# The product of probabilities and values with V held in the array: four 32-column strips instead of eight weight loads, and 64-row scores

## The chip, the cores and the metric

The kernel runs on one core of a Trainium2 chip. The metric is the device time of one launch in microseconds (us). Unless ns is written, all times here are in us. TensorE multiplies (PE in the profile; PEld are its weight loads), ScalarE evaluates exponentials (ACT), VectorE (DVE) and GpSimd (POOL) do the rest of the arithmetic, SyncE (SP) and POOL issue the transfers.

## The reference, cut to what matters

A transformer block with adaptive layer norm and its whole backward pass: 2048 tokens, width 512, 32 heads of 16, a hidden layer of 1792. The change touches the forward attention alone:

```python
H = 32
Dh = D // H
qkv = (x @ wqkv).reshape(B, S, 3, H, Dh).transpose(2, 0, 3, 1, 4)
q, k, v = qkv[0], qkv[1], qkv[2]
scores = einsum('bhqd,bhkd->bhqk', q, k) * Dh ** -0.5
p = softmax(scores, axis=-1)
o = einsum('bhqk,bhkd->bhqd', p, v)
return o.transpose(0, 2, 1, 3).reshape(B, S, D) @ wo
```

The forward also has `x + ga * A(h)`, a second norm, `r = relu(h @ w1 + b1)`, `(r * r) @ w2 + b2`; then come the gradients of all inputs and weights.

## The kernel before, in words

**Stages.** `phase_fwd` holds the whole forward and the part of the backward that goes by token (the MLP gradients); `phase5` is the backward attention; `phase6` the last weight gradients. PE and SP follow the order in which the program is written throughout; in the forward loop ACT and DVE do too. POOL does so in the opening, and is ordered by the scheduler from the second part of the loop on.

**Tiling of the forward attention.** Queries are cut into four chunks of 512 (`qc`), the 32 heads into eight groups of four (`g`), a group into two pairs (`jp`), and the keys into sixteen blocks of 128 (`kb`). One pair, one key block and one query chunk make a *unit*: 1024 units in all. A unit is

- two score matmuls (L388, or L354 in the opening): the 128 keys of a block are the stationary operand (`KTq`, four heads in four 32-row strips, each 16 rows of head and 16 of zeros), the 512 queries of one head move (`QTm`, all rows but those of the head zero). The result is one tile `st` of two PSUM banks; there are two such tiles, so the scores of a unit wait until ACT has read those of the unit two before;
- one exponential over both heads on ACT (L391, L357), 128 partitions by 1024, into `pu`, of which there are six;
- eight matmuls with `pu` stationary (L322, `pv`): each loads 128 by 128 of `pu` and moves 17 columns of `Vaug` (16 of V and one of ones, which gives the softmax's sum). The result has tokens on partitions: 2 heads by 4 token tiles by 17 columns of one bank, `accbank`, of which there are two.

After a pair's last block, two reciprocals (L329) and two multiplications (L330) on DVE turn `accbank` into rows of `O32`.

**What sets the order.** `pend` holds the eight-matmul products of past units; a unit may execute those that are two units old. Beside them the *background* runs: generators that emit one matmul per `yield` (queries and keys of the next group in chunk 0, `gen_qkv`; the MLP of the chunk before, `gen_mlp`, in chunks 1 to 3). `Background.step` adds a rate (1.2 in chunk 0, 1.14 later) to a credit and runs matmuls while the credit is positive; a generator can ask for a hold of some units with `("wait", n)`. `room` (L398) lets fewer products run in a unit that has more background. `bg.until(mark)` runs background up to a mark at once.

**Loads.** `load_q` (L299) issues two DMAs on POOL's queue that refill the queries of the next pair in the one set of four `QTm` tiles; a refill waits for the score matmuls that still read the tile. `load_k` does so for the keys.

**The opening** (L339 to L364) lays the first group's 32 units between the norm, the projections and the transposes that they need (`gen_open`). Its first queries lie in two extra tiles `QTo`.

**The end of the loop.** After the last unit the rest of `pend` runs (L419), `take_o` (L1156) casts `O32` to bf16, and `last_chunk` does the fourth chunk's MLP, forward and backward, with PE as the engine that is kept full. What background is left (three quarters of the second MLP product of chunk 2, `fc2`, L1255 and the bias L1257) is laid in by `bg.take` and, at L828, by `bg.drain()`, before the transposes of the second norm's output (L782) and the first MLP product (L838).

Of the kernel before, what the change touches and what calls it, by code (L numbers as in the profile page):

```python
# [9 lines left out]
BF16 = mybir.dt.bfloat16  # L10
F32 = mybir.dt.float32
ACT = mybir.ActivationFunctionType
ALU = mybir.AluOpType
AX = mybir.AxisListType
PSUM = bass.MemoryType.PSUM
# [4 lines left out]
P = 128  # L20
DH = 16
# [14 lines left out]
class Background:  # L36
# [13 lines left out]
    def next(self):  # L50
        while self.gens:
            r = next(self.gens[0], None)
            if r is not None:
                if isinstance(r, tuple):
                    self.mark = r[0]
                    self.seen.add(r[0])
                return r
            self.gens.pop(0)
        return None

    def plan(self, rate):
        return 0 if self.hold or not self.gens else max(0, math.ceil(min(self.credit + rate, 2.0)))

    def step(self, rate):
        if self.hold:
            self.hold -= 1
            return
        self.credit = min(self.credit + rate, 2.0)
        while self.gens and self.credit > 0:
            r = self.next()  # L70
            if r is None:
                break
            if isinstance(r, tuple):
                self.hold = r[1]
                break
            self.credit -= max(r, 0.25)

    def until(self, mark):
        while mark not in self.seen:
# [26 lines left out]
class K:  # L106
# [160 lines left out]
    def phase_fwd(self):  # L267
# [5 lines left out]
        tc, nc, pp = self.tc, self.nc, self.pp  # L273
# [15 lines left out]
        fw = self.open_pool("fw", bufs=1)  # L289
# [2 lines left out]
        pup = self.open_pool("fwp", bufs=6)  # L292
        self.mps = self.open_pool("mps", bufs=2, space=PSUM)
        stp = self.open_pool("fwst", bufs=2, space=PSUM)
        accp = self.open_pool("fwacc", bufs=2, space=PSUM)
        O32 = self.ra.tile([P, 4, D], F32, name="O32")
        QTm = [fw.tile([P, 512], BF16, name=f"QTm{j}") for j in range(4)]

        def load_q(qc, g, jp):  # L299
            with tc.high_priority():  # L300
                for j in (2 * jp, 2 * jp + 1):
                    nc.gpsimd.dma_start(QTm[j][32 * j:32 * j + 32, :], self.QTq_d[g, 32 * j:32 * j + 32, 512 * qc:512 * (qc + 1)])  # L302

        def load_k(qc, g):
            if qc == 0:
                return self.KT_next
            t = kp.tile([P, S], BF16, name="KTq")
            with tc.high_priority():
                nc.gpsimd.dma_start(t[:], self.KTq_d[g])
            return t  # L310

        SPAN, PVT = 4.15, 0.12
        order = [(qc, g, jp) for qc in range(SC) for g in range(NQ) for jp in range(2)]
        bg = Background()
        bg.add(self.gen_qkv(kp))
        pend = []

        def pv(w):
            (u, a, sub) = w
            (n, qc, g, jp, kb, acc, pu) = u  # L320
            h = 4 * g + 2 * jp + a
            nc.tensor.matmul(acc[:, a, sub, :], lhsT=pu[:, a, sub * P:(sub + 1) * P], rhs=Vaug[:, kb, h, :],  # L322
                             start=(kb == 0 and a == 0 and sub == 0), stop=False, skip_group_check=True)
            if kb < ST - 1 or (a, sub) != (1, 3):
                return
            st0 = 4 * qc
            for a in range(2):
                h = 4 * g + 2 * jp + a
                nc.vector.reciprocal(self.rl[:, st0:st0 + 4, h], acc[:, a, :, DH])  # L329
                nc.vector.tensor_tensor(O32[:, :, h * DH:(h + 1) * DH], acc[:, a, :, 0:DH],  # L330
                                        self.rl[:, st0:st0 + 4, h:h + 1].to_broadcast([P, 4, DH]), ALU.mult)
            if (g, jp) == (NQ - 1, 1) and qc < SC - 1:
                bg.add(self.gen_mlp(qc, self.take_o(qc, O32)))

        KT = kp.tile([P, S], BF16, name="KTq")
        self.late = []
        self.cur_g = 0
        es = ExitStack()
        es.enter_context(tc.manual_schedule(engines=ALL))  # L339
        QTo = []  # L340
        first = self.gen_open(Vaug, KT, QTm, QTo, stp, bg)
        next(first)
        accs = []
        for n in range(2):
            accb = accp.tile([P, 512], F32, name="accbank")
            accs.append(accb[:, 0:8 * (DH + 1)].rearrange("p (a s e) -> p a s e", a=2, s=4))
        units = [(n, 4 * s + k) for s in range(SC) for n in range(2) for k in range(4)]
        for i, (n, kb) in enumerate(units):
            if i == len(units) // 2:
                bg.until(1)  # L350
                load_q(*order[2])
            stt = stp.tile([P, 2, 512], F32, name="st")
            for a in range(2):
                nc.tensor.matmul(stt[:, a, :], lhsT=KT[:, kb * P:(kb + 1) * P], rhs=(QTm[2 + a] if n else QTo[a])[:],  # L354
                                 start=True, stop=True)
            pu = pup.tile([P, 2, 512], BF16, name="pu")
            nc.scalar.activation(pu[:], stt[:], ACT.Exp, scale=self.scale)  # L357
            u = (n, 0, 0, n, kb, accs[n], pu)
            next(first)
            pend.extend((u, a, sub) for a in range(2) for sub in range(4))  # L360
            while len(pend) > 24:
                pv(pend.pop(0))
        next(first)
        es.close()  # L364
# [1 line left out]
        late, self.late = self.late, None  # L366
        bg.until(-1)
        KT = self.KT_next
        for n, (qc, g, jp) in list(enumerate(order))[2:]:
            if (qc, g, jp) == (1, 0, 0):  # L370
                bg.drain()
                es.close()
                self.close_qkv()
                self.open_mlp()
                bg.add(self.gen_weights())
            accb = accp.tile([P, 512], F32, name="accbank")
            acc = accb[:, 0:8 * (DH + 1)].rearrange("p (a s e) -> p a s e", a=2, s=4)
            self.cur_g = g
            for kb in range(ST):
                if kb == (5 if qc == 0 and jp == 1 else 1) and n + 1 < len(order):  # L380
                    if n < 2 * NQ - 1 and jp == 1:
                        bg.until(g + 1)
                    load_q(*order[n + 1])
                    if jp == 1:
                        KTn = load_k(*order[n + 1][:2])
                stt = stp.tile([P, 2, 512], F32, name="st")
                for a in range(2):
                    nc.tensor.matmul(stt[:, a, :], lhsT=KT[:, kb * P:(kb + 1) * P], rhs=QTm[2 * jp + a][:],  # L388
                                     start=True, stop=True)
                pu = pup.tile([P, 2, 512], BF16, name="pu")  # L390
                nc.scalar.activation(pu[:], stt[:], ACT.Exp, scale=self.scale)  # L391
                u = (n, qc, g, jp, kb, acc, pu)
                now = n * ST + kb
                pend.extend((u, a, sub) for a in range(2) for sub in range(4))
                if late:
                    late.pop(0)()
                rate = 1.14 if qc else 1.2
                room = int((SPAN - 2 - bg.plan(rate)) / PVT)  # L398
                while pend:
                    age = now - max(pend[0][0][0] * ST + pend[0][0][4], 2 * ST - 2)  # L400
                    if age < 2 or (room <= 0 and age < 4):
                        break
                    pv(pend.pop(0))
                    room -= 1
                bg.step(rate)
            if jp == 1 and n + 1 < len(order):
                if n < 2 * NQ - 1:
                    bg.until(-(g + 1))
                KT = KTn
        bg.until(f"fc2_{SC - 2}")  # L410
# [4 lines left out]
        for k in range(2):  # L415
            t = self.mk.tile([P, D], BF16, name="x0", bufs=2)
            nc.gpsimd.dma_start(t[:], self.io["A_x"][0].rearrange("(st p) d -> p st d", p=P)[:, ST - 4 + k, :])
            x0s.append(t)
        while pend:  # L419
            pv(pend.pop(0))  # L420
        O_b = self.take_o(SC - 1, O32)
        for name in ("fwacc", "fwst", "fwp", "fwk", "fw"):
            self.close_pool(name)
        self.last_chunk(bg, O_b, x0s, O32)

    def gen_open(self, Vaug, KT, QTm, QTo, stp, bg):

        tc, nc, io = self.tc, self.nc, self.io
        S, D, H, NQ, ST, DT, SC = self.S, self.D, self.H, self.NQ, self.ST, self.DT, self.SC
# [32 lines left out]
            load_x(s4)  # L462
        nc.sync.dma_start(self.wmod[:, :, 2 * D:6 * D], wmod_v[:, :, 2 * D:6 * D])
        nc.gpsimd.memset(Vaug[:, :, :, DH:DH + 1], 1.0)
        nc.vector.memset(QTm[0][:], 0.0)
        self.silu_c(ps)
        QTo.extend(sa_.tile([P, 512], BF16, name=f"QTo{j}") for j in range(2))
        for t in QTo + QTm[1:]:
            nc.vector.memset(t[:], 0.0)
        for t in self.wpad0 + wpads[::-1]:  # L470
            nc.scalar.memzero(t[:])
# [1 line left out]
        def warm(n):  # L473
            w = stp.tile([P, 2, 512], F32, name="st")
            for _ in range(n):
                nc.tensor.matmul(w[:, 0, :], lhsT=self.ones_b[:], rhs=QTm[0][:], start=True, stop=True)

        warm(12)
        xhat1 = tokens("auT", "xhat1")
# [54 lines left out]
        def fm(*a, **k):  # L534
            for _ in self.gen_fm(ps, *a, **k):
                pass
# [22 lines left out]
        warm(4)  # L559
        fm(1, 0, 0, dst=KT[:, 0:512])  # L560
        pad0(0)
        fm(0, 0, 0, masked=QTo + QTm[2:])
        warm(2)
        for st in range(4, 8):
            stat(st)
# [1393 lines left out]
```

## Time and profile before

| what | us |
|---|---|
| median of 3 runs | 2509.76 (2506.19 to 2510.69) |
| the profiled execution: its time, its span | 2511.14, 2509.0 |
| opening up to the first exponential | 16.7 |
| opening, 32 units | 47.5 |
| chunk 0, the other 224 units | 208.1 |
| chunk 1, 256 units | 238.4 |
| chunk 2, 256 units | 235.3 |
| chunk 3, 256 units | 235.5 |
| last chunk's MLP and the dense weight gradients (from 981.5 to 1170) | 188.5 |
| backward attention (1170 to 2400) | 1230 |
| rest | 109 |

The stages were cut at the starts of exponentials, read from the timeline. A profile shows one execution. A row of the groups has the source line, the engine, the operation, output and inputs, shape, count, then busy time and mean duration of one. Matmuls overlap in the array, so a mean of 377 ns does not say that one starts every 377 ns: starts are read from the timeline. The granted clock of TensorE was 1.00 in nearly all stages, 0.99 in chunk 1.

### The profile page before, as it was taken

To read this page: it belongs to the slowest core of one execution; us is meant where nothing else is said; L and a number is where in the kernel's file an instruction comes from. 1 tells how busy PE (TensorE), PEld (TensorE's weight loads), DVE (VectorE), ACT (ScalarE), POOL (GpSimd) and SP (SyncE) were. 2 spreads that over 40 slices of the span, in tenths; PEclk is the share of its full clock that TensorE was granted. 3 is DMA by queue.
4 is the path that set the end of the run, shared out by engine and by line. 5 is a ranking of instruction groups with operands and counts; after the bars stand their busy time and mean duration, and the time that the engine had idled before them with its cause. 6 is when DMAs were issued, how large, how long until landed. Compare 5 with 4: busy or idle time off the path is not lost.

```text
span 2509.0 us, 68721 instructions
## 1 busy us (share of the span) xinstructions
PE 2438.6 (97%) x26695; PEld 1080.0 (43%) x26695; DVE 1709.6 (68%) x3519; ACT 2295.0 (91%) x3789; POOL 716.4 (29%) x1289
## 2 busy tenths in 40 slices
PE   8999999999999999999999999999999999999998
PEld 4555555555555554573333333333333333333343
DVE  6222322422332344677999999999999999999957
ACT  7999999999999997534999999999999999999935
POOL 2344531220131022245222222222222222222223
PEclk9999999999999999999999999999999999999999
DMA  4688661441243044598999999999999999999997
GB/s 166 133 180 208 170 121 50 129 100 39 99 115 90 23 131 138 122 199 214 236 215 227 224 221 228 223 222 221 229 222 222 230 223 222 225 226 232 233 191 208
DMA packets 1260526, 445.78 MB, mean 178 GB/s; under 512 B 1204052, under 2 KB 1228246, under 8 KB 1260198
## 3 DMA queue, kind: packets, MB, share of 16 engines
q1 hardware_dynamic: 1219654, 336.29, 70.7%
q0 software_dynamic: 38464, 104.04, 13.6%
q8 instruction: 209, 3.42, 0.6%
q10 hardware_dynamic: 2080, 1.05, 0.1%
q14 instruction: 119, 0.97, 0.1%
HBM read 75.83 MB, written 64.49 MB: 56 GB/s over the span
## 4 chain that ended last, share of the span: by engine, by line
PE 58%; ACT 27%; DMA 7%; issue 4%; DVE 3%; POOL 1%; SPq 0%; DVEq 0%; ACTq 0%; POOLq 0%
ACT pu L391 18%; PE st L1601 17%; PE acckv L1459 8%; PE st L388 8%; ACT pu L1604 7%; PE accq L1484 5%; DMA dsT<-ds 3%; PE accbank L322 3%; PE dps L1050 2%; PE pps L1237 2%; PE st L1559 1%; PE dp L1522 1%; PE dp L1652 1%; DVE ds L1526 1%; DMA keep<-ds 1%
## 5 line engine op out<-in xcount | busy, mean ns | idle before, releaser
L1526 DVE TENSOR_TENSOR ds<-dp,pu 128x512 bf16<-128x512 f32 x1920 | 1181.7, 684 | 25.1 <-PE dp L1522 19.1
L1604 ACT ACTIVATE pu<-st 128x512 bf16<-128x512 f32 x2048 | 1072.7, 661 | 30.1 <-PE st L1601 21.3
L391 ACT ACTIVATE pu<-st 128x1024 bf16<-128x1024 f32 x992 | 912.2, 1077 | 5.1 <-PE st L388 4.9
L388 PE MATMUL st<-QTm,KTq 128*128 128x512 bf16 x1984 | 588.4, 377 | 20.0 <-ACT pu L391 6.0
L322 PEld LDWEIGHTS <-pu 128*128 128x128 bf16 x8192 | 347.3, 96 | 236.3 <-issue 3.2
L1522 PE MATMUL dp<-kvm,q 64*128 64x512 bf16 x1024 | 364.1, 384 | 1.5 <-DVE ds L1526 0.7
L1522 PE MATMUL dp<-kvm,dOTg 64*128 64x512 bf16 x1024 | 361.8, 384 | 0.5 <-DVE ds L1526 0.4
L322 PE MATMUL accbank<-Vaug,pu 128*128 128x17 bf16 x8192 | 357.7, 171 | 1.2 <-ACT Vaug L522 0.9
L1601 PE MATMUL st<-kvm,q 64*128 64x512 bf16 x1024 | 351.6, 381 | 6.0 <-ACT pu L1604 0.2
L1601 PE MATMUL st<-kvm,QTg 64*128 64x512 bf16 x1024 | 350.6, 381 | 6.8
L388 PEld LDWEIGHTS <-KTq 128*128 128x128 bf16 x1984 | 188.2, 96 | 177.5 <-issue 125.6
L1535 POOL TENSOR_TENSOR ds<-junk,pu 128x512 bf16<-128x512 f32 x64 | 73.8, 1153 | 372.2 <-ACT junk L1534 302.4
L1459 PE MATMUL acckv<-ds,Qg 128*16 128x512 bf16 x1024 | 176.0, 382 | 0.2
L1459 PE MATMUL acckv<-pu,dOg 128*16 128x512 bf16 x1024 | 175.9, 382 | 0.0
L1459 PE MATMUL acckv<-ds,q 128*16 128x512 bf16 x1024 | 175.8, 382 | 0.0
L1459 PE MATMUL acckv<-pu,q 128*16 128x512 bf16 x1024 | 175.8, 382 | 0.0
L1535 POOL TENSOR_TENSOR ds<-csq,pu 128x512 bf16<-128x512 f32 x64 | 73.8, 1154 | 349.6 <-ACT csq L1534 271.5
L302 POOL DMA_DIRECT2D QTm<-QTq_d x124 | 63.8, 516 | 341.5 <-PE st L388 319.9
L1601 PEld LDWEIGHTS <-q 64*128 64x128 bf16 x1024 | 66.9, 94 | 159.6 <-issue 144.0
L1601 PEld LDWEIGHTS <-QTg 64*128 64x128 bf16 x1024 | 67.0, 94 | 158.2 <-issue 141.3
L329 DVE RECIPROCAL rl<-accbank 128x4 f32<-128x4 f32 x128 | 23.0, 179 | 159.0 <-PE accbank L322 158.8
L1522 PEld LDWEIGHTS <-q 64*128 64x128 bf16 x1024 | 89.8, 93 | 56.7 <-issue 50.4
(390 smaller groups left out, 3197.0 us busy)
## 6 DMA issues: line engine op xcount, KB each, us to landing
KTq<-KTq_d POOLq DMA_DIRECT2D x24, 512.0 KB, 3.8
duT_d<-auT POOLq DMA_DIRECT2D x3, 1792.0 KB, 7.6
aT_d<-rT POOLq DMA_DIRECT2D x3, 1792.0 KB, 11.0
KTq_d<-KTq SPq DMA_DIRECT2D x32, 128.0 KB, 2.1
QTq_d<-ev_fm SPq DMA_DIRECT2D x32, 128.0 KB, 4.3
ktm_d<-ev_tm POOLq DMA_DIRECT2D x32, 128.0 KB, 2.5
VTq_d<-vT POOLq DMA_DIRECT2D x4, 1024.0 KB, 6.2
dx<-dx_d SPq DMA_DIRECT2D x16, 256.0 KB, 5.3
```

Of the source, the lines that this page charges most:

```text
L302: nc.gpsimd.dma_start(QTm[j][32 * j:32 * j + 32, :], self.QTq_d[g, 32 * j:32 * j + 32, 512 * qc:512 * (qc + 1)])
L322: nc.tensor.matmul(acc[:, a, sub, :], lhsT=pu[:, a, sub * P:(sub + 1) * P], rhs=Vaug[:, kb, h, :], start=(kb == 0 and a == 0 and sub == 0) ...
L388: nc.tensor.matmul(stt[:, a, :], lhsT=KT[:, kb * P:(kb + 1) * P], rhs=QTm[2 * jp + a][:], start=True, stop=True)
L391: nc.scalar.activation(pu[:], stt[:], ACT.Exp, scale=self.scale)
L1050: nc.tensor.matmul(pt[:], lhsT=a[st], rhs=g_tm[:, st, :], start=(st == 0), stop=(st == ST - 1))
L1459: nc.tensor.matmul(acckv[r:r + DH, :], lhsT=T[n][:, ib, col:col + DH], rhs=src[:, a, :], start=(ib == 0), stop=(ib == ST - 1))
L1484: nc.tensor.matmul(accq[r:r + 32, o:o + 256], lhsT=T["K"][:, 4 * c + sub, col:col + 32], rhs=v[:, r // 32 % 2 * 2:r // 32 % 2 * 2 + 2, 4 * ...
L1522: nc.tensor.matmul(dp[:], lhsT=T["dOT"][rd, ib * P:(ib + 1) * P], rhs=masked["VT"][a][rd, 512 * c:512 * (c + 1)], start=True, stop=True)
L1526: nc.vector.tensor_tensor(dsg[:, i, a], dp[:], pu[:, a, :], ALU.mult)
L1535: nc.gpsimd.tensor_tensor(dsg[:, i, 1], f[:], pu[:, 1, :], ALU.mult)
L1601: nc.tensor.matmul(stt[:], lhsT=T["QT"][rs, q], rhs=masked["KT"][a][rs, c0:c0 + 512], start=True, stop=True)
L1604: nc.scalar.activation(pu[:, a, :], stt[:], ACT.Exp, scale=self.scale)
```

## The change

The unit, the exponential and the order of the key blocks stay. What is written anew:

1. **P times V.** For a key block, once both pairs' exponentials exist, four matmuls run with `Vaug` stationary (128 by 17) and `pu` moving (128 by 512). Their outputs lie on partitions 0 to 16, 32 to 48, 64 to 80 and 96 to 112 of one bank, one strip of 32 columns of the array for each head. So a group of four heads, not a pair, is the turn of the loop; there are 32 turns of 32 units.
2. **O turned.** The strips hold O by head dimension. After a group's last block DVE copies the bank to `csq` (`OTs`, 128 by 512 fp32, zeros in the unused rows, which two memsets set once), and four fp32 matmuls with `csq` stationary and 68 columns of the identity moving put tokens back on partitions, in the same bank. They wait in `fin` and run one per even unit of the next group. Then one reciprocal (128 by 16) and one multiplication (128 by 256) on DVE.
3. **Order.** A product of a block runs in odd units, one per pair of units; a turning matmul in an even one. `Background.step` gets `most`: 1 in a unit with a product or a turning matmul (and then only if the credit is above 1.5), else 2; the credit may reach 3. `plan` and `room` go.
4. **Queries.** Two sets of four tiles instead of one set and `QTo`; the next group's are loaded a group ahead, four DMAs at once.
5. **64-row scores from chunk 1 on.** Heads 0 and 2 share one query tile, heads 1 and 3 another. A unit's two score matmuls use rows 0 to 63 and rows 64 to 127 of keys and queries. In chunk 0 they stay at 128 rows. `gen_open` differs only in the query tiles.

```diff
-    def step(self, rate):
+    def step(self, rate, most):
...
-        self.credit = min(self.credit + rate, 2.0)
-        while self.gens and self.credit > 0:
+        self.credit = min(self.credit + rate, 3.0)
+        while self.gens and self.credit > (0 if most > 1 else 1.5) and most > 0:
...
+            most -= r
...
+        def unit(KT, n, kb, jp):
+            stt = stp.tile([P, 2, 512], F32, name="st")
+            for a in range(2):
+                r, t = (slice(64 * a, 64 * a + 64), QTm[n % 2][jp]) if n >= NQ else (slice(0, P), QTm[n % 2][2 * jp + a])
+                nc.tensor.matmul(stt[:, a, :], lhsT=KT[r, kb * P:(kb + 1) * P], rhs=t[r, :], start=True, stop=True)
+            pu = pup.tile([P, 2, 512], BF16, name="pu")
+            nc.scalar.activation(pu[:], stt[:], ACT.Exp, scale=self.scale)
+            return pu
...
         def pv(w):
-            nc.tensor.matmul(acc[:, a, sub, :], lhsT=pu[:, a, sub * P:(sub + 1) * P], rhs=Vaug[:, kb, h, :],
-                             start=(kb == 0 and a == 0 and sub == 0), stop=False, skip_group_check=True)
...
+            if kb < ST:
+                for j in range(4):
+                    nc.tensor.matmul(acc[32 * j:32 * j + DH + 1, :], lhsT=Vaug[:, kb, 4 * g + j, :], rhs=pus[j % 2][:, j // 2, :] if qc else pus[j // 2][:, j % 2, :],
+                                     start=(kb == 0), stop=(kb == ST - 1))
+                if kb == ST - 1:
+                    nc.vector.tensor_copy(OTs, acc[:])
+                return
+            sub = kb - ST
+            o = acc[:, 0:16 * (DH + 1)].rearrange("p (s j e) -> p s j e", s=4, j=4)
+            nc.tensor.matmul(o[:, sub], lhsT=OTs[:, sub * P:(sub + 1) * P],
+                             rhs=self.ident_f[:].rearrange("p (j e) -> p j e", e=32)[:, :, 0:DH + 1],
+                             start=True, stop=True, skip_group_check=True)
...
+                if fin and now > fin[0][0] and i % 2 == 0:
+                    pv(fin.pop(0))
+                    most = 1
+                elif pend and now >= pend[0][0] + 2:
+                    pv(pend.pop(0))
+                    most = 1
+                else:
+                    most = 2
+                bg.step(rate, most)
```

## The prediction

> **What bounds the kernel now.** I read first the busy time by stage, then the costliest groups, then the timeline inside a chunk. By stage (columns: PE, weight loads, DVE, ACT, POOL busy, clock, DMA):
>
> ```profile
> 64.20:272.30 208.10, 201.40 (x2504) 114.24 (x2502) 50.16 (x141) 206.43 (x225) 91.77 (x172) 1.00 0.75 173
> 746.00:981.50 235.50, 232.22 (x2841) 128.92 (x2839) 76.42 (x222) 235.28 (x257) 46.94 (x81) 1.00 0.33 88
> ```
>
> In the loop ACT is busy for 206.43 of 208.10 us and for 235.28 of 235.50. PE is nearly full too, so which of them sets the pace must come from the timeline:
>
> ```profile
> 599.09 7.51 ACT L391 ACTIVATE pu<-st 128x1024 bf16<-128x1024 f32 x8
> ...
> 600.22 0.59 PE L388 MATMUL st<-QTm,KTq 128*128 128x512 bf16 x2
> ...
> 600.65 0.37 PE L322 MATMUL accbank<-Vaug,pu 128*128 128x17 bf16 x9
> ...
> 600.88 0.38 PE L1212 MATMUL pps<-fT,w 128*128 128x512 bf16 x1
> ...
> 601.14 0.59 PE L388 MATMUL st<-QTm,KTq 128*128 128x512 bf16 x2
> ```
>
> Eight exponentials take 7.51 us and one lasts 1.09, so they come (7.51 - 1.09) / 7 = 0.917 apart. PE needs less for a unit: the two scores start 0.214 apart and leave the array free 0.43 after the first; nine products take 600.65 to 600.88, 0.025 each; one background matmul 0.214. That is 0.86, and the next scores start at 0.92: PE waits. **ACT is the bound**, at 0.917 x 256 = 234.8 us a chunk. Losses against that are small: chunk 0 2.7 us (224 units), chunk 1 3.6, chunk 2 0.5, chunk 3 0.7. So relieving PE can give 7.5 us at the very most, and what matters is whether the new order makes PE late.
>
> How late may PE be? The exponential that begins at 600.00 ends at 601.09; scores follow at 601.14, the second at 601.36 ends at 601.73 (0.377), the exponential on them starts at 601.83. With the shortest exponential (1.017) the way round is 0.05 + 0.214 + 0.377 + 0.10 + 1.017 = 1.758 for two units, against 2 x 0.917 = 1.833. **Scores may be 0.075 late**; beyond that ACT stands still.
>
> **What the products cost.** Before, sixteen of 0.0245 per pair of units, 0.39, spread evenly. The strips are not in the forward, but the backward has them, and 64-row pairs beside them:
>
> ```profile
> 1701.86 0.37 PE L1601 MATMUL st<-kvm,QTg 64*128 64x512 bf16 x1
> 1701.87 0.39 PE L1522 MATMUL dp<-kvm,dOTg 64*128 64x512 bf16 x1
> 1702.18 0.39 PE L1459 MATMUL acckv<-ds,Qg 128*16 128x512 bf16 x2
> 1702.19 0.39 PE L1459 MATMUL acckv<-pu,dOg 128*16 128x512 bf16 x2
> 1702.40 0.38 PE L1459 MATMUL acckv<-ds,Qg 128*16 128x512 bf16 x2
> 1702.41 0.38 PE L1459 MATMUL acckv<-pu,dOg 128*16 128x512 bf16 x2
> 1702.72 0.39 PE L1601 MATMUL st<-kvm,QTg 64*128 64x512 bf16 x1
> ```
>
> Four strips start within 0.01, the next four 0.22 later: four at the price of one. Two 64-row matmuls also go together (1701.86, 1701.87). But from scores to strips 0.32 passes, and from strips to scores 0.32, where 0.22 would do: **each change of the array's shape costs about 0.095**. Full-width to strips has the same price (0.309 at 2411, L1652 and L1661, where 0.214 would do). A block's product therefore costs 0.095 + 0.226 + 0.095 = 0.416: as much as the 0.39 it replaces.
>
> [...]
>
> **Chunk 0 (128-row scores).** The product sits in one slot now, the odd unit. In the order in which the changed program's instructions stand on PE, 82 of chunk 0's 112 odd units after the opening hold scores, product and one background matmul: 0.428 + 0.416 + 0.214 = 1.058. Over ACT's 0.917 by 0.141, less 0.075 of slack: 0.066 lost. The even units (scores and one or two background matmuls, 0.64 to 0.86) win the lateness back, so it recurs: 82 x 0.066 = **+5.4**. Bounds: 0.06 a change gives no loss and takes 1.5 of the present 2.7 away; 0.13 a change gives 82 x 0.14 = 11.5. I take the measured 0.095.
>
> **Chunks 1 to 3.** A 64-row pair takes 0.212, and its second score ends 0.21 sooner, so the slack is 0.28. Odd unit: 0.212 + 0.095 + 0.226 + 0.095 + 0.214 + 0.095 = 0.937; even: 0.212 + 0.095 + 0.428 + 0.095 = 0.83. Nothing is lost; the little that is lost to bunched matmuls goes. The one large loss stays: at 319.31 the first L1212 waits for a transfer (fT from xh), 2.8 us and 0.5 for the lower clock after it. Thirteen units lie between the last L1190 and this matmul in both orders. I take **-0.8**; bounds -4.2 (that wait gone as well) and +6 (changes at 0.13).
>
> **Turning O.** A 128x128 fp32 matmul (L1000) starts its successor 0.22 later; with 68 columns I take 0.21 (bounds 0.11, two passes by columns, and 0.38, two weight loads of 0.190). In an even unit with one background matmul: 0.428 + 0.21 + 0.214 = 0.85, below 0.917: hidden by ACT. If that cover went it would be 128 x 0.21 = 27 us. DVE loses 4 x (0.179 + 0.224) = 1.6 a group and gains a copy of 0.69 and some 0.6; it is a quarter busy: nothing.
>
> **POOL and SP.** POOL waited 319.9 us in all for scores to release a query tile; with two sets this goes. Nobody on the path waited for POOL there (1.1 us on PE in all), so nothing; the DMAs are as many. SP's order is the same but for neighbours.
>
> **The opening.** PE-bound (44.91 busy of 47.5): 16 x (0.416 - 0.39) = +0.4. Two more query memsets (0.27 each) stand on DVE before the first statistics, which follow without idle time: +0.5. The two PSUM memsets fall in DVE's idle 2 us there. **+0.9**, bounds 0 and 2.
>
> **The tail.** Before:
>
> ```profile
> 981.57 0.37 PE L322 MATMUL accbank<-Vaug,pu 128*128 128x17 bf16 x8 [0.32 <-ACT pu L391]
> ...
> 982.80 1.43 DVE L1161 CAST O_b<-O 128x512 bf16<-128x512 f32 x4
> ...
> 983.28 0.73 PE L782 MATMUL tp<-ident,O_b 128*128 128x128 bf16 x8
> ...
> 993.17 1.89 PE L1255 MATMUL pps<-w,rT 128*128 128x512 bf16 x8
> ...
> 995.31 0.62 PE L782 MATMUL tp<-ident,xh 128*128 128x128 bf16 x8
> ...
> 999.05 12.26 PE L838 MATMUL pps<-fT,w 128*128 128x512 bf16 x56 [0.52 <-DVE fT L783]
> ```
>
> From the last exponential (981.5) to the casts (982.80) is 1.3. After: strips 0.43, copy 0.73, four fp32 matmuls back to back 1.1, reciprocal 0.2, multiplication 0.42 (between the 64-element row, 0.224, and a 512-element one, 0.69), with hand-overs about 3.1: +1.8, and nothing covers it. Second, less background fits into the loop, as a unit with a product takes at most one: in the changed order 40 matmuls of fc2 stand behind the last score, in the old 24. The 16 more all stand in the drain between 993.17 and 995.31, which PE does at full rate: 16 x 0.214 + 0.2 for the second bias = 3.6; some 0.8 of it is hidden, as the transposes after 995.31 now find ACT idle and need not wait for xh (996.5). After that PE is full. **+4.6**, bounds +1.8 (all hidden) and +6.
>
> **Sum.** 0.9 + 5.4 - 0.8 + 4.6 = +10.1 on the profiled execution's 2511.14: 2521.2. That execution is 1.4 above the median, so **2520** is forecast, 0.4% slower.
>
> **Rivals.**
> - *The changes of shape cost nothing beside full-width matmuls* (0.2). An odd unit is then 0.428 + 0.226 + 0.214 = 0.87, chunk 0 gains 1.5 instead of losing 5.4, and the tail is all that is left: 2509.8 + 0.9 - 1.5 - 0.8 + 4.6 = 2513, no change. It decides as soon as an odd unit of chunk 0 stays below 0.917 + 0.075 = 0.99. For: the rows of the backward are mostly between 64 rows and strips. Against: the 0.309 at 2411.
> - *Faster* (0.06): as above, and the wait of chunk 1 goes (-3.3) and the drain is hidden (-2.8): 2507; with the opening unharmed and the last ACT losses gone 2504.
> - *The clock falls* (0.1). In chunks 1 to 3 some units have no background; there PE now works for 0.21 and 0.6 of each 0.917. After the 2.8 us without work at 318, scores took 0.43 instead of 0.214 (320.11 to 320.97 for two). If such stretches bring that, about four units at double price (some +0.9 each) follow each of about six stretches: +20, 2540. Against: 69% work in such units before left the clock at 1.00.
> - *Strips run one after another* (0.02): 0.86 for 0.226 in each of 512 pairs, PE-bound: over 2700. The backward's rows exclude it nearly.
>
> The forecast has 0.62. The range 2509 to 2533 leaves out the fastest and the clock's cases. About 0.2% (5 us) is what a measurement of this kernel tells from no change: faster 0.06, same 0.2, slower 0.74.
>
> **What would show it.** In chunk 0 exponentials come in turns 0.917 and about 0.98 apart where an odd unit has background; PE starts strips 0.31 after the second score; ACT in chunks 2 and 3 stays at 0.917; the casts of O start about 3.1 after the last exponential; the drain has 23 or so fc2 matmuls. It is wrong if chunk 0 takes 208 again, if the strips' starts are far apart, or if the clock of chunks 1 to 3 is below 0.97.

## The result and the profile after

The changed kernel takes **2537.05 us** (2532.45 to 2541.69), the kernel before 2508.99 on the same chip: a ratio of 1.0104 (95% interval 1.0088 to 1.0121), 28 us slower where 10 were forecast. The profiled execution took 2541.69 (span 2539.9), 30.9 more than the span before. By landmarks of the two timelines:

| stretch | before | after | more | forecast |
|---|---|---|---|---|
| up to the first exponential | 16.74 | 18.97 | +2.2 | } +0.9 |
| opening, 32 units | 47.47 | 45.76 | -1.7 | } |
| chunk 0, 224 units | 208.10 | 213.87 | +5.8 | +5.4 |
| chunks 1, 2, 3 (to the last exponential's start) | 708.14 | 719.41 | **+11.3** | -0.8 |
| last exponential to the first fc1 (L838, now L854) | 18.60 | 25.15 | +6.5 | +4.6 |
| from there to the backward's first exponential | 169.26 | 167.63 | -1.6 | 0 |
| backward attention, first to last exponential | 1215.17 | 1221.44 | **+6.3** | 0 |
| rest | 125.54 | 127.69 | +2.2 | 0 |

The busy times by stage of the changed kernel (columns: PE, weight loads, DVE, ACT, POOL busy, clock, DMA), one row a chunk:

```profile
64.73:278.60 213.87, 206.88 (x1208) 76.89 (x1207) 50.21 (x106) 210.67 (x226) 92.72 (x175) 1.00 0.70 167
278.60:518.92 240.32, 220.76 (x1362) 72.14 (x1362) 75.77 (x175) 236.07 (x258) 71.62 (x98) 0.93 0.42 108
518.92:758.51 239.59, 224.93 (x1352) 73.85 (x1350) 75.36 (x188) 235.63 (x258) 47.90 (x84) 0.97 0.30 82
758.51:999.24 240.73, 227.47 (x1349) 74.18 (x1349) 74.92 (x181) 236.27 (x257) 44.52 (x76) 0.96 0.29 82
```

Chunk 0 keeps the clock at 1.00 and ACT waits there. In chunks 1 to 3 the clock is 0.93, 0.97 and 0.96, where it was 1.00 at 746 to 981 before. The PE timeline of chunk 2 shows how it falls and what that costs:

```profile
577.98 0.39 PE L324 MATMUL st<-QTm,KTq 64*128 64x512 bf16 x2 [0.52 <-ACT pu L326]
578.30 0.39 PE L334 MATMUL accbank<-pu,Vaug 128*17 128x512 bf16 x4
578.89 0.39 PE L324 MATMUL st<-QTm,KTq 64*128 64x512 bf16 x2 [0.20 <-ACT pu L326]
...
585.45 0.69 PE L341 MATMUL accbank<-ident_f,csq 128*128 128x68 f32 x2
586.08 0.61 PE L324 MATMUL st<-QTm,KTq 64*128 64x512 bf16 x2
586.62 0.61 PE L334 MATMUL accbank<-pu,Vaug 128*17 128x512 bf16 x4
587.15 0.61 PE L324 MATMUL st<-QTm,KTq 64*128 64x512 bf16 x2
...
589.56 0.59 PE L1228 MATMUL pps<-fT,w 128*128 128x512 bf16 x1 [1.17 <-DMA fT<-xh]
590.08 0.61 PE L324 MATMUL st<-QTm,KTq 64*128 64x512 bf16 x2
590.61 0.61 PE L334 MATMUL accbank<-pu,Vaug 128*17 128x512 bf16 x4
591.15 0.61 PE L1228 MATMUL pps<-fT,w 128*128 128x512 bf16 x1
591.69 0.61 PE L324 MATMUL st<-QTm,KTq 64*128 64x512 bf16 x2
...
595.68 0.39 PE L324 MATMUL st<-QTm,KTq 64*128 64x512 bf16 x2
```

Up to 581 the background pauses, and a unit is a score pair and, in every second unit, a product: the brackets show PE waiting 0.52 and 0.20 for ACT in turn. Units without background are called *thin* from here on. At 581.7 the record of the clock goes to one half, and matmuls stand 0.54 apart instead of 0.32. A pair of thin units still hides under ACT then (three steps of 0.54 in 1.83), but not where a turning matmul joins in (585.45): from 581.2 on six exponentials come 1.06 to 1.17 apart, 1.1 lost in all. When fc1 comes back (589.56, after 1.17 of waiting for its transfer) a unit takes 590.08 to 591.69 = 1.61 instead of 0.917, until the clock returns at 595.4. The granted clock is halved in six such stretches of chunks 1 to 3, each 3.4, 6.8, 13.7 or 17.1 long: multiples of 3.41. Against ACT's 0.917 a unit the three chunks lose some 16 us, all of it in the 70 or so units in or just behind those stretches (some 17.6; the others, together, lose nothing). Not all of that is the clock: PE's two waits for fc1's transfer (0.84 ahead of 328.4, and the 1.17) lie there too.

### The profile page after: what moved, and what is told of

Same layout as the page of the kernel before. It is cut to its first block, busy times and chain, and to the rows that moved or that the text cites. A ratio compares the mean times of both kernels' runs of the same rounds, so it can differ in the third digit from the quotient of the medians.

```text
span 2539.9 us, 56823 instructions
## 1 busy us (share of the span) xinstructions
PE 2433.5 (96%) x20807; PEld 875.5 (34%) x20807; DVE 1710.2 (67%) x3363; ACT 2302.9 (91%) x3789; POOL 713.3 (28%) x1289
## 4 chain that ended last, share of the span: by engine, by line
PE 45%; ACT 37%; issue 8%; DMA 7%; DVE 3%; POOL 1%; DVEq 0%; ACTq 0%; POOLq 0%; SPq 0%
ACT pu L326 28%; PE st L1617 16%; PE acckv L1475 8%; ACT pu L1620 7%; PE accq L1500 5%; DMA dsT<-ds 4%; PE st L324 2%; PE dps L1066 2%; DVE ds L1542 1%; PE st L1575 1%; PE dp L1538 1%; PE dp L1668 1%; PE pps L647 1%; PE st L1763 1%; PE accbank L334 1%
## 5 line engine op out<-in xcount | busy, mean ns | idle before, releaser
L326 ACT ACTIVATE pu<-st 128x1024 bf16<-128x1024 f32 x1024 | 951.1, 1123 | 23.8 <-PE st L324 22.2
L324 PE MATMUL st<-QTm,KTq 64*128 64x512 bf16 (+1 forms) x2048 | 463.6, 394 | 52.4 <-ACT pu L326 47.2
L324 PEld LDWEIGHTS <-KTq 64*128 64x128 bf16 (+1 forms) x2048 | 141.2, 94 | 306.9 <-issue 254.4
L334 PE MATMUL accbank<-pu,Vaug 128*17 128x512 bf16 x2048 | 208.0, 396 | 0.5 <-ACT pu L326 0.5
L1500 PE MATMUL accq<-dsT,keep 128*32 128x256 bf16 x1632 | 104.8, 278 | 4.8 <-DMA dsT<-ds 4.8
L1538 PEld LDWEIGHTS <-dOTg 64*128 64x128 bf16 x1024 | 89.2, 93 | 55.9 <-issue 50.0
```

Of the source, the lines that this page charges most:

```text
L324: nc.tensor.matmul(stt[:, a, :], lhsT=KT[r, kb * P:(kb + 1) * P], rhs=t[r, :], start=True, stop=True)
L334: nc.tensor.matmul(acc[32 * j:32 * j + DH + 1, :], lhsT=Vaug[:, kb, 4 * g + j, :], rhs=pus[j % 2][:, j // 2, :] if qc else pus[j // 2][:, ...
L1500: nc.tensor.matmul(accq[r:r + 32, o:o + 256], lhsT=T["K"][:, 4 * c + sub, col:col + 32], rhs=v[:, r // 32 % 2 * 2:r // 32 % 2 * 2 + 2, 4 * ...
L1538: nc.tensor.matmul(dp[:], lhsT=T["dOT"][rd, ib * P:(ib + 1) * P], rhs=masked["VT"][a][rd, 512 * c:512 * (c + 1)], start=True, stop=True)
```

## The experiments

Ten kernels ran. All were timed beside the kernel before, whose medians in the three sets were 2512.78 (e_same, e_fill, e_full, e_rows0), 2510.90 (e_before, e_rowsonly, e_rate, e_best) and 2512.32 (e_q, e_best2). The table has, from each profile, the halved stretches that begin in chunks 1 to 3, what each chunk lost against ACT's 0.917 a unit, the tail (last exponential to first fc1) and the backward (first to last exponential).

| kernel | median | halved | chunk 0 | 1 | 2 | 3 | tail | backward |
|---|---|---|---|---|---|---|---|---|
| before | 2508.99 | 1 | 2.8 | 3.8 | 0.6 | 0.7 | 18.6 | 1215.2 |
| e_before | 2511.76 | 0 | 2.2 | 2.2 | 0.7 | 1.0 | 18.6 | 1216.9 |
| e_rowsonly | 2519.88 | 7 | 2.4 | 6.3 | 3.4 | 3.4 | 18.8 | 1214.5 |
| after | 2537.05 | 6 | 8.5 | 5.7 | 4.9 | 5.8 | 25.2 | 1221.4 |
| e_same | 2542.76 | 7 | 8.5 | 5.2 | 6.5 | 4.7 | 25.1 | 1219.8 |
| e_fill | 2527.56 | 1 | 8.5 | 5.2 | 1.0 | 0.9 | 25.3 | 1222.1 |
| e_q | 2528.10 (one) | 2 | 8.5 | 3.2 | 3.4 | 0.7 | 23.9 | 1220.4 |
| e_full | 2544.58 | 1 | 8.5 | 6.9 | 11.4 | 8.0 | 23.6 | 1219.1 |
| e_rows0 | 2536.71 | 6 | 6.1 | 11.1 | 6.1 | 3.8 | 23.9 | 1218.6 |
| e_rate | 2534.76 | 8 | 8.5 | 15.6 | 2.9 | 6.1 | 21.4 | 1219.4 |
| e_best | 2516.93 | 1 | 3.0 | 2.6 | 0.4 | 6.0 | 18.2 | 1218.8 |
| e_best2 | 2512.92 | 1 | 3.0 | 2.3 | 0.1 | 0.3 | 17.2 | 1221.2 |

**Thin units filled.** `step` returns how much background it ran; where it ran none, PE gets something to do.

```diff
-                bg.step(rate, most)
+                if not bg.step(rate, most) and qc:
+                    w = self.mps.tile([P, 512], F32, name="pps")
+                    for _ in range(most):
+                        nc.tensor.matmul(w[:], lhsT=self.ones_b[:], rhs=QTm[n % 2][jp][:], start=True, stop=True)
```

> As the changed kernel, but in every unit of chunks 1 to 3 in which no background ran, PE runs one or two extra 128x512 matmuls of ones into a background bank that nobody reads; the output is unchanged. Theory 1 (the missing time of chunks 1 to 3 is the lower clock that follows units with little PE work): the clock of chunks 1 to 3 is 0.99 or more, each chunk loses at most 0.8 us against ACT's 0.917 x 256, and the kernel is 11 to 16 us faster than the changed one. Theory 2 (the changes of array shape, or PE's waits, cost more there than reckoned): PE has more to do and nothing is gained, 0 to 8 us slower than the changed one. If both hold in part, it lies between.

Measured: 2527.56, ratio 1.0051 (1.0032 to 1.0069), 15.2 less than the changed kernel beside it. By stage:

```profile
277.22:517.04 239.82, 226.89 (x1430) 74.85 (x1443) 76.67 (x175) 235.15 (x258) 71.02 (x96) 0.99 0.43 109
517.04:752.75 235.71, 224.30 (x1370) 74.15 (x1384) 75.29 (x188) 234.93 (x258) 48.43 (x86) 1.00 0.34 84
752.75:988.60 235.85, 223.82 (x1367) 73.92 (x1382) 74.84 (x181) 235.06 (x257) 44.33 (x76) 1.00 0.30 84
```

Chunks 2 and 3 are as before the change but for 0.2 to 0.4, with *more* work on PE: theory 1 holds, theory 2 falls. Chunk 1 still loses 5.2: 3.8 in three units around 304, where PE stands for 2.8 us ahead of the chunk's first wo matmul and the clock falls for one window, and 1.3 ahead of fc1. The loop gives 9.2 (719.40 to 710.22 by the two profiles), the opening 1.4: its code is the same, but this profile has no fall of the clock there (first exponential at 17.60, in e_same at 18.96). The rest is spread over stages whose code is the same.

**Are strips the cause, or 64-row scores?** Two kernels have one of them each.

```diff
-        pup = self.open_pool("fwp", bufs=6)
+        pup = self.open_pool("fwp", bufs=4)
...
-                r, t = (slice(64 * a, 64 * a + 64), QTm[n % 2][jp]) if n >= NQ else (slice(0, P), QTm[n % 2][2 * jp + a])
+                r, t = slice(0, P), QTm[n % 2][2 * jp + a]
```

> As the changed kernel, but with 128-row scores in all chunks (two sets of four query tiles, paid for with four instead of six exponential tiles); the strips stay. In units without background PE then works 0.43 in each 0.917 and 0.226 in every second: 59% instead of 35%. Theory 1 (too little PE work lowers the clock): no halved clock in chunks 1 to 3, but some 325 odd units with background now cost 1.058 as in chunk 0, 0.066 lost in each, so chunks 1 to 3 lose 20 to 24 us in place of 15.6, and the kernel is 3 to 9 us slower than the changed one. Theory 2 (the strips themselves, not the thin units, cost the time): the clock falls as often as in the changed kernel, and 0.066 per odd unit comes on top: 18 to 25 us slower.

The second is the kernel before with this, and the loads and head numbers that go with it:

```diff
-                    nc.tensor.matmul(stt[:, a, :], lhsT=KT[:, kb * P:(kb + 1) * P], rhs=QTm[2 * jp + a][:],
-                                     start=True, stop=True)
+                    r, t = (slice(64 * a, 64 * a + 64), QTm[jp]) if qc else (slice(0, P), QTm[2 * jp + a])
+                    nc.tensor.matmul(stt[:, a, :], lhsT=KT[r, kb * P:(kb + 1) * P], rhs=t[r, :], start=True, stop=True)
```

> The kernel before with only the 64-row scores from chunk 1 on (heads j and j + 2 of a group in one unit); the products stay as they were, sixteen 17-column matmuls per pair of units, and so does the planner. In a unit without background PE then works 0.212 + 0.196 of 0.917 us, 44%; in the changed kernel it was 35%, and there the clock fell after windows of 3.41 us with 31 to 40% of PE work, and stayed after windows of 41% and more. Theory 1 (the share of PE work decides): the clock is halved in chunks 1 to 3 only after the wait for a transfer near 318 us, chunks 1 to 3 lose 3 to 6 us as before, and the kernel is within 4 us of the one before. Theory 2 (64-row scores lower the clock, whatever the share): six or more halved stretches as in the changed kernel, 8 to 16 us slower than before.

By stage, strips with 128-row scores first, then 64-row scores with the old products:

```profile
278.68:520.26 241.58, 228.13 (x1337) 84.81 (x1363) 75.73 (x175) 240.41 (x258) 70.84 (x96) 1.00 0.42 111
520.26:766.34 246.08, 236.30 (x1326) 86.66 (x1351) 75.33 (x188) 241.99 (x257) 48.13 (x84) 0.99 0.31 80
766.34:1009.30 242.96, 234.61 (x1326) 86.47 (x1350) 74.86 (x181) 241.46 (x256) 44.21 (x76) 1.00 0.29 81
```

```profile
271.92:512.86 240.94, 236.32 (x2835) 111.94 (x2835) 78.02 (x221) 235.99 (x258) 70.29 (x96) 0.88 0.47 111
512.86:750.94 238.08, 235.22 (x2830) 110.51 (x2828) 73.35 (x222) 235.41 (x257) 48.51 (x83) 0.96 0.34 85
750.94:989.40 238.46, 235.22 (x2841) 110.74 (x2839) 76.52 (x222) 235.64 (x257) 47.03 (x81) 0.96 0.34 87
```

With strips and 128-row scores the clock holds but for one window after a wait for fc1's transfer, and chunks 1 to 3 lose 26.3, of which 3.9 lie at that wait and in that window: 22.4 remain. Two more waits for fc1's transfer (at 326 and 833) have 2.5 of these, so some 20 are left for the odd units, the lower end of the 20 to 24 expected. So the price of a change of shape was about right. In time the kernel was only 1.8 slower than the changed one beside it (3 to 9 expected).

The other kernel went *against* theory 1 as I had put it: seven halved stretches at "44%", and 9 us. It looks as theory 2 said; but theory 2 says "whatever the share", and with fillers (e_fill) the same 64-row scores leave the clock at 1.00 in chunks 2 and 3. What was wrong is how I counted. Its thin units:

```profile
545.30 0.39 PE L389 MATMUL st<-QTm,KTq 64*128 64x512 bf16 x2 [0.23 <-ACT pu L391]
545.62 0.36 PE L322 MATMUL accbank<-Vaug,pu 128*128 128x17 bf16 x8
546.21 0.48 PE L389 MATMUL st<-QTm,KTq 64*128 64x512 bf16 x2 [0.23 <-ACT pu L391]
546.63 0.38 PE L322 MATMUL accbank<-Vaug,pu 128*128 128x17 bf16 x8
547.13 0.61 PE L389 MATMUL st<-QTm,KTq 64*128 64x512 bf16 x2
```

A 17-column product occupies PE for 0.0245, but 17 of 512 columns at 0.214 are 0.007. Counted by columns that move, a thin unit has 0.212 + 8 x 0.007 of 0.917: 29%, not 44%. I then counted all profiles so, in the 3.41 us (the stretches' unit) ahead of each fall of the clock in the loop: all 44 falls followed a share of 0.38 or less (a pair, or four strips, that start together counted once), none a higher one. The converse holds nearly: of some 3,070 other windows of 3.41 us at full clock, laid end to end from the falls, about 30 had 0.38 or less (0.32 at the lowest) without a fall. The window ahead of 561.3 is one of them in the changed kernel (0.36), while in e_same, the same program, the clock fell there. By occupied time there is no such order: PE was occupied for 0.98 of the window ahead of the fall at 310.9 here.

**A smaller filler**, to bound that share from above:

```diff
+                if not bg.step(rate, most) and qc and jp == 0:
+                    w = self.mps.tile([P, 512], F32, name="pps")
+                    nc.tensor.matmul(w[:, 0:256], lhsT=self.ones_b[:], rhs=QTm[n % 2][jp][:, 0:256], start=True, stop=True)
```

> The changed kernel with a smaller filler: one 128x256 matmul of ones in every second unit of chunks 1 to 3 in which no background ran; the output is unchanged. Counting what PE streams (0.214 us for 512 columns, so 0.007 for 17), a pair of thin units has 2 x 0.212 + 0.226 + 0.107 = 0.757 in 1.833 us, 41%; it was 35% in the changed kernel and 29% with 64-row scores and the old products, and both fell; 53% in the kernel before and 59% with 128-row scores and strips, and both stayed. If the limit lies below 41%: one halved stretch in chunks 1 to 3 at most, and the 11 to 15 us of the larger filler come with this one too (about 2526). If it lies above: six or so stretches as in the changed kernel, about 2538.

One timed execution: 2528.10. Two falls, at 324.4 and 583.8, each just after a wait for fc1's transfer (1.19 and 0.95 us) had begun; none in a stretch of thin units alone. So thin units with 41% held the clock, nearly as expected (two falls, not one), and 0.107 us of PE work in every second thin unit does what the large filler does: the loop behind chunk 0 takes 710.36, with the large one 710.22.

**64-row scores in chunk 0 too.**

```diff
-                r, t = (slice(64 * a, 64 * a + 64), QTm[n % 2][jp]) if n >= NQ else (slice(0, P), QTm[n % 2][2 * jp + a])
+                r, t = slice(64 * a, 64 * a + 64), QTm[n % 2][jp if n >= NQ else jp + 2 * a]
...
-rhs=pus[j % 2][:, j // 2, :] if qc else pus[j // 2][:, j % 2, :],
+rhs=pus[j % 2][:, j // 2, :],
```

> As the changed kernel, but with 64-row scores in chunk 0 as well (heads j and j + 2 of a group in one unit). An odd unit of chunk 0 with one background matmul then takes PE 0.212 + 0.226 + 0.214 and three changes of shape of 0.095: 0.937 instead of 1.058, inside ACT's 0.917 and the slack. Theory 1 (the 5.8 us of chunk 0 are odd units with 128-row scores, product and background): chunk 0 loses 1.5 to 3.5 us in place of 8.5, and the kernel is 4 to 7 us faster than the changed one, if the clock of chunk 0, where background runs in nearly every unit, stays at 1.0. Rival (changes of shape cost more than 0.095 when a third one comes into the unit): chunk 0 loses 8 or more again. The opening is PE-bound: two 64-row scores side by side save 0.2 of each of its units, less two changes of shape, so it stays within 1 us.

```profile
62.13:273.59 211.46, 190.93 (x1186) 64.46 (x1207) 50.29 (x106) 207.14 (x225) 93.43 (x176) 0.96 0.71 169
273.59:519.38 245.79, 225.74 (x1352) 71.98 (x1362) 75.03 (x175) 237.27 (x257) 70.92 (x97) 0.88 0.43 106
```

Outside halved stretches chunk 0 loses 2.3, inside the 1.5 to 3.5 of theory 1: the 5.8 were the odd units. But its condition fails: the clock now falls in chunk 0 as well (0.96), at 125 and 187, where the background pauses after a change of group, and at 268, behind its last matmul of the chunk; 3.8 come back as loss. Chunk 1 loses 11.1: the fall at 268 lasts to 306, and 3.3 of the 11.1 are not the clock alone, as PE stands for 2.76 ahead of the chunk's first wo matmul (301.63). Beside the changed kernel it is 6 us faster.

**More background per unit**, for the tail:

```diff
-                rate = 1.14 if qc else 1.2
+                rate = 1.28 if qc else 1.2
```

> The changed kernel with the rate at which chunks 1 to 3 take background raised from 1.14 to 1.28 a unit. In the order of its instructions no matmul of fc2 is left behind the last score, where the changed kernel has 40 with their bias matmuls. Theory 1 (the tail's 3.7 us between the first wo matmul and the first transpose of xh are those matmuls of fc2): that stretch takes 8.6 to 9.2 us instead of 12.24, and the tail is 3 to 4 us shorter. Rival (the stretch is bound by the vector work on x_l, and the matmuls lay beside it): it takes 11 or more. Chunks 1 to 3 lose about as much as in the changed kernel (13 to 20 us), as thin units stay and a few more come at the chunks' ends, where the background is now done early. In all 0 to 5 us faster than the changed kernel.

The tail of the changed kernel, then of this one:

```profile
1007.81 1.02 PE L833 MATMUL pps<-wo,fT 128*128 128x512 bf16 x4 [0.46 <-DVE o L1276]
...
1014.25 2.11 PE L1271 MATMUL pps<-w,rT 128*128 128x512 bf16 x9
1016.29 0.38 PE L1273 MATMUL pps<-b2gb_b,ones_b 1*128 1x512 bf16 x1
1016.60 3.19 PE L1271 MATMUL pps<-w,rT 128*128 128x512 bf16 x14
1019.73 0.39 PE L1273 MATMUL pps<-b2gb_b,ones_b 1*128 1x512 bf16 x1
1020.05 0.62 PE L798 MATMUL tp<-ident,xh 128*128 128x128 bf16 x8
```

```profile
1013.27 4.94 PE L833 MATMUL pps<-wo,fT 128*128 128x512 bf16 x12
1018.04 1.03 PE L827 MATMUL dps<-fT,W2gbT 128*128 128x512 bf16 x4
1018.90 1.03 PE L833 MATMUL pps<-wo,fT 128*128 128x512 bf16 x4
1019.77 1.02 PE L827 MATMUL dps<-fT,W2gbT 128*128 128x512 bf16 x4
1020.75 0.40 PE L798 MATMUL tp<-ident,xh 128*128 128x128 bf16 x4
```

From the first wo to the first transpose of xh 12.24 become 7.48, below the 8.6 expected, though PE runs at half speed there (twelve wo matmuls in 4.94): theory 1. The clock is halved from 1000.6 to 1017.7; no fc2 fills PE there while O is turned. Chunks 1 to 3 lose 24.6, more than the 13 to 20 expected. Eight halved stretches are one part: background that is done early leaves more thin units. Another is a wait of PE, 3.1 ahead of the first wo matmul of chunk 1 (305.39), which costs 3.7. In the median the kernel is within the changed one's spread (1.009, 1.0055 to 1.0125).

**All together**: the edits of e_rows0, e_rate and e_fill (without its `and qc`), and this, where `fill(k, t)` runs k of the large fillers on tile `t`:

```diff
+            if not pend and len(fin) == 4:
+                fill(4, QTm[0][0])
             pv((pend or fin).pop(0))
+        fill(8, QTm[0][0])
...
             yield from self.gen_weights_1()
-            yield ("wait", 4)
+            yield ("wait", 9)
```

> The changed kernel with what the runs point to: 64-row scores in chunk 0 too; in every unit without background one or two extra 128x512 matmuls of ones that nobody reads, in chunk 0 as well; rate 1.28; 4 and 8 such matmuls beside the last copy of O and its turning; and 9 instead of 4 units of pause ahead of the first fc1 of chunk 1, for the transfer that cost 2.8 us. The output is unchanged. Expected against the changed kernel if the terms add: opening -1, chunk 0 -5 to -6, chunks 1 to 3 -15 for the clock and -2 to -3 for the transfer, tail -4: 26 to 30 us faster, 2509 to 2515 where the kernel before gives about 2512, so equal to it. If the clock is not the cause, or extra PE work costs ACT time, it stays above 2520.

It came to 2516.93 (1.0022, 1.0007 to 1.0037), just above the 2509 to 2515 expected: opening, chunk 0, chunks 1 and 2 as expected, the tail 3 better; chunk 3 lost 6.0, most of it in one wait (columns: total, times, longest):

```profile
PE pps L1219 <- DMA fT<-O_b: 4.4, 1, 4.4
```

The turned O is ready later than before, its transfer takes 10.7, and a pause of nine units is 8.3: with the faster background the first wo matmul stands on PE ahead of the scores.

So the pauses were made longer:

```diff
-        yield ("wait", 9 if sc else 14)
+        yield ("wait", 13 if sc else 18)
...
-            yield ("wait", 11)
+            yield ("wait", 12)
...
-                rate = 1.28 if qc else 1.2
+                rate = 1.3 if qc else 1.2
```

> The combined kernel again, with longer pauses of the background for the two transfers that PE still waited for: 18 and 13 units instead of 14 and 9 ahead of the first wo matmul of a chunk (the transfer from the casts of O takes 10.7 us, more than 9 units of 0.917), 12 instead of 11 ahead of fc1, and a rate of 1.3. In the combined kernel these waits cost 2.5 us in chunk 1 and 4.7 and 1.1 in chunk 3. If they go and nothing comes in their place: 6 to 8 us less than its 2517, so 2509 to 2511, equal to the kernel before within 0.2%. If the waits move to the next transfer: 2514 or more.

2512.92 beside 2512.32: 1.0004 (0.9990 to 1.0017), the same as the kernel before, though some 2 above the 2509 to 2511 expected. The loop has the small losses of the table's last row; the 1.0 to 1.2% that the change cost are undone, and nothing is won. Its one fall of the clock is instructive:

```profile
311.50 0.39 PE L327 MATMUL st<-QTm,KTq 64*128 64x512 bf16 x2
311.82 0.39 PE L337 MATMUL accbank<-pu,Vaug 128*17 128x512 bf16 x4
312.15 0.35 PE L1161 MATMUL pps<-sbT_b,w 128*128 128x1 bf16 x8
312.44 0.39 PE L327 MATMUL st<-QTm,KTq 64*128 64x512 bf16 x2
312.76 0.45 PE L1161 MATMUL pps<-sbT_b,w 128*128 128x1 bf16 x12
...
314.27 0.61 PE L327 MATMUL st<-QTm,KTq 64*128 64x512 bf16 x2
```

PE hardly waits here (some 0.1 us in the 3.41 ahead); its background are matmuls that move one column each, and the clock falls at 313.8 all the same.

**The two kernels again**, without an edit.

> The changed kernel once more, unaltered, beside the others. Its backward is the same code as before, yet in the profile of the changed kernel it took 6 us longer. Theory A (that is spread between executions): the backward of this profile lies elsewhere, by several us, and the median is 2532 to 2541. Theory B (the change reaches into the backward): the backward takes 1221 us again, against 1215 before. In either case the clock is halved again in stretches of 3 to 17 us in chunks 1 to 3, as it comes from the program's own order.

> The kernel before, unaltered, as a second profile of its own. In the profiles of the changed kernel and of its variants the backward, whose code is the same, took 1218.6 to 1222.1 us from its first exponential to its last, in the one profile of the kernel before 1215.2. Theory A (spread between executions): a second profile of the kernel before lies in 1215 to 1222 too, above 1217. Theory B (the change reaches into the backward): 1215 again, within 1. The rest of the profile should repeat within 1 us per chunk.

In the changed kernel the halved stretches repeat in kind and partly in place: in e_same they begin at 292, 302, 329, 384, 561, 582 and 817, in the first profile at 292, 326, 387, 582, 800 and 817. The chunks of the kernel before repeat within 0.6 us, but for chunk 1, which is 1.6 shorter: the wait for fc1's transfer at 318 (1.64) isn't followed by a fall this time. On the backward neither theory holds cleanly: 1219.8 for the changed kernel, 1216.9 for the one before. Over all profiles the kernels with the old products took 1214.5 to 1216.9 (three), those with strips 1218.6 to 1222.1 (nine): the sets don't overlap, so some 4 us belong to the change. They show in part in PE's waits for one transfer (columns as above), before and after:

```profile
PE accq L1484 <- DMA dsT<-ds: 3.8, 8, 0.9
```

```profile
PE accq L1500 <- DMA dsT<-ds: 7.9, 10, 1.6
```

In the three it is 3.2 to 5.4, in the nine 5.3 to 9.2. Why that transfer should be later in code that is the same **stays open**; the place of the query tiles is not it, as e_full has them elsewhere and still takes 1219. The rest behind the backward (+2.2) lies inside what the twelve profiles spread over, 122.2 to 128.8.

## Why the prediction was wrong

- **Step that failed: "Chunks 1 to 3. Nothing is lost", -0.8.** Measured +11.3. The step took the clock as 1.00 throughout; it was 0.93, 0.97 and 0.96, two of them below the 0.97 that the prediction named as a sign of being wrong. With fillers that held the clock (e_fill) the loop took 9.2 less. Outside the halved stretches the step holds (nothing lost in 700 units). The rival *the clock falls* had the right place and mechanism (thin units, then background at half speed), but got a chance of 0.1 and was left out of the range. The reason against it, "69% work in such units before left the clock at 1.00", says nothing about the new units, which have half of that: the value asked about lay far outside the rows. The trace held rows that pointed the other way, from the kernel before:

```profile
319.31 1.01 PE L1212 MATMUL pps<-fT,w 128*128 128x512 bf16 x2 [1.87 <-DMA fT<-xh]
320.11 1.06 PE L388 MATMUL st<-QTm,KTq 128*128 128x512 bf16 x2
```

PE waited 1.87 there (the prediction's 2.8 without work is what ACT lost), and in the 3.41 us ahead of the fall at 318.8 columns still moved for 0.3 of the time. So the clock had fallen with PE at work.
- **The rival's price**, +20, was too high: +11 was paid, as much of a halved stretch lies in thin units, where ACT hides it (of the stretch from 387.2 to 400.8 the first 12 units lose 0.6, the two behind them 0.8). That its 2540 comes so near 2537 is partly chance: the tail's further 1.9 and the backward's 6.3, which no term of it held, made up for the difference.
- **The prediction counted PE's time, and the falls of the clock here follow another count.** By moved columns a thin unit fell from 53% to 35%; 64-row scores alone (e_rowsonly) bring it to 29% and cost 9 us, strips alone (e_full) leave it at 59%, with one fall, behind a wait. Those two, with the small filler at 41%, order by columns and not by occupied time (44% fell, 41% stayed). A count by occupied array instead (strips use 17 of 32 columns) orders them as well: 53% before and in e_full, 36% with the small filler, 30% in the changed kernel, 29% in e_rowsonly. No run tells these two counts apart.
- **Chunk 0, +5.4: right** (+5.8), for the reason given. The odd unit shows it: strips 0.31 after the second score, the next matmul 0.33 after them.

```profile
140.99 0.59 PE L324 MATMUL st<-QTm,KTq 128*128 128x512 bf16 x2
...
141.51 0.39 PE L334 MATMUL accbank<-pu,Vaug 128*17 128x512 bf16 x4
...
141.84 0.39 PE L647 MATMUL pps<-xm1T,wpad 128*128 128x512 bf16 x1
...
142.06 0.59 PE L324 MATMUL st<-QTm,KTq 128*128 128x512 bf16 x2
```

From 140.99 to 142.06 the unit takes 1.07, where 1.058 was reckoned. That the changes of shape cost nothing is excluded. The loss comes in fewer and larger steps than forecast: around there three exponentials come 0.90 to 0.92 apart and the fourth 1.02, not 0.917 and 0.98 in turn.
- **The tail, +4.6: mechanism right, size short by 1.9.** The drain has its 23 matmuls and takes 3.66 more, of which the 0.8 taken off as hidden was not hidden; the casts of O start 3.1 after the last exponential ends, as said. But the transposes of O start 1.44 after the first of those casts, before 0.48: six fc2 matmuls stand ahead of them on PE, 2.39 from 1001.42 to 1003.81; the clock is halved there, from 1001.6 to 1005.0.
- **Opening, +0.9: right in sum** (+0.5), but by luck: the 32 units became 1.7 faster, and the start 2.2 slower. Some 1.4 of the 2.2 goes with a halved clock from 11.7 to 15.1, which e_fill's profile, with the same code there, doesn't have.
- **The turning of O** is hidden as said at full clock: 0.28 a matmul, where 0.21 was taken (620.92 to 621.20 in the changed kernel). At half clock it is not (581 to 588).
- **The backward, 0:** about +4, cause open.

No window of 3.41 us ahead of a fall in the loops was idle throughout: columns moved for 0.12 of the time or more (0.12 in e_best, behind its wait of 4.4), for 0.3 or more in most (0.31 to 0.38 ahead of the six falls of the changed kernel), and ahead of the fall at 313.8 in e_best2 PE stood for some 0.1 us in all.

## What to carry to other kernels

Relieving an engine that is not the bound can cost time: here TensorE fell to half clock where it moved columns for little more than a third of the time (35% in the changed kernel's thin units), and the next dense stretch paid. So when a change makes matmuls cheaper, look at the thinnest stretch of the loop, not at the mean, and count columns moved, not time occupied (by occupied time 44% fell here and 41% held); 0.1 us of matmuls that nobody reads, in every second thin unit, held the clock but for two waits for a transfer. And a value that lies outside everything the trace has tried deserves a wide range and a real chance, above all where one row hints at a cliff.

## What was unexpected of the hardware

- The clock halved with PE at work; all 44 falls in the loops followed 3.41 us with 0.38 or less of moved columns, also where PE was occupied nearly all the time by 17-column or 1-column matmuls. About 30 of some 3,070 other windows had so little and no fall.
- The halved stretch at 581.7 lasted as long as the thin units did and 5.8 us of dense work more (589.6 to 595.4), where each unit took 1.5 to 1.6 instead of 0.917.
- A change between full-width and strip or 64-row shapes costs about 0.1 us beside full-width matmuls too (from start to start, in the changed kernel: 0.31 into strips and 0.33 out of them around 141.51, 0.32 from full width to a 64-row pair at 595.36, where 0.21 would do): some 20 us in three chunks of strips among 128-row scores.
